# Second layer of a two-layer kernel: one of its Strassen products split by Strassen once more, and one sum formed by an adding DMA

## Chip, cores, metric

The kernel runs on one core of one Trainium2 chip. The time is device microseconds of one execution; before the change it is 2410.37 us, the median of 3 runs (2410.23 to 2410.72). The profile is one more execution of the same kernel, with a span of 2408.5 us on TensorE, VectorE (DVE in the profile), ScalarE (ACT), GpSimd (POOL) and the DMA queues.

## Reference

A causal depthwise convolution with 7 taps (softmax-normalised, one set for each of 8 heads), then a feed-forward layer with a hard-swish gate. All data is float32.

```python
batch, seq, d_model = (8, 4096, 192)         # 32768 tokens
d_ff = 2048

x = conv(x, softmax(weight))                 # (32768, 192)
h = x @ w_in                                 # (32768, 2048)   "first layer"
g = h * clip(h + 3.0, 0.0, 6.0) / 6.0        # the gate
out = g @ w_out                              # (32768, 192)    "second layer"
```

## The kernel before

The tokens go in 32 blocks of 1024. In a block the kernel keeps d_ff on the partitions, 16 chunks of 128. For the second layer it treats g as a 2 by 2 matrix: A11, A21, A12, A22 are d_ff half 0 or 1 (second digit) and token half 0 or 1 (first digit), each 8 chunks (NP) of 128 partitions by 512 tokens (N). w_out is a 2 by 2 matrix as well: d_ff halves by halves of the 192 output columns, 96 columns each, which are 3 column tiles (NQ) of 32 (QS). Strassen's scheme in Winograd's form makes 7 products of these quarters in place of 8, from sums S1 to S4 of the A and T1 to T4 of the B.

```python
g = cst.tile([P, NP, 2, G, N], F32, name="g")
g4 = g[:].rearrange("p c h k n -> p c (h k) n")
A11, A21, A12, A22 = (g4[:, :, j] for j in range(4))
S2, S3, S4 = A11, A21, A12                   # these sums are formed in place
psum = ps.tile([P, 2 * 4, N], F32, name="psum")     # 8 banks
...
def gate(out, r6, h):                        # L321, VectorE
    nc.vector.scalar_tensor_tensor(out=out, in0=r6, scalar=1.0, in1=h, op0=ALU.min, op1=ALU.mult)

def g_of(c, group, k):                       # where a gate writes
    return g[:, c, k, k if group == OWN else 1 - k]
```

The first layer (also in a Strassen form) runs in UNITS = 4 units of two chunks. A unit's steps stand in a plan as words: L or U is the lower or the upper half of the array (k = 0 or 1), P1 to P7 and K11 to K22 are matmuls, F1, CE, AF, AD copies and additions between PSUM banks, R a ReLU on ScalarE (L317), G a gate on VectorE (L321). The results of a unit are a and f (group OWN) and b and d (group OTHER), with a and b in chunk 2u and f and d in chunk 2u + 1. A step with ' belongs to the unit before, so that the fifth plan holds only what is left of unit 3.

```python
FIRST = """
    LP1 UP1 LP5 UP5 LF1 UF1 UP5+ LP6 LCE UCE UP6 LP2 UCE+ UK11 LAF LK11 UAF X UP2 LP7
    LRa UP7 LK12 URa LAD UP3 LP3 UAD LGa UK12 LK22 LRf UGa UK22 LK21 URf LGf LRd UK21
""".split()
...
OTHERS = """
    UP1 UGf' LP1 URd' LGd' LP4' UP4' UGd' LF1 LP5 UP5 UF1 LP6 UP6 LCE UCE LP2 UK11 LAF
    LRb' UAF LK11 UP2 URb' LGb' LP7 UP7 URa UGb' LRa LK12 UP3 LAD LP3 UAD UK12 UGa LK22
    UK22 LRf LGa URf LK21 UK21 LGf LRd
""".split()
PLANS = [FIRST, SECOND] + [OTHERS] * (UNITS - 1)

def h_phase(left):
    for u, plan in enumerate(PLANS):
        for step in plan:
            ...
        if u:
            g_sums(nc.gpsimd, (1, 3), range(2 * u - 2, 2 * u), 2)

def g_sums(engine, which, slots, width):     # L498
    forms = {
        1: (S1, A21, A22, ALU.add), 3: (S3, A11, A21, ALU.subtract),
        2: (S2, S1, A11, ALU.subtract), 4: (S4, A12, S2, ALU.subtract),
    }
    ...                                      # one tensor_tensor for each `width` chunks
```

The second layer. mm makes one matmul for each chunk (L437): the weights are 128x32, the array is split in 4 column tiles (j), and four such streams run side by side, one in each column tile.

```python
prod = {
    1: (A11, B11), 2: (A12, B21), 3: (S4, B22), 4: (A22, T4),
    5: (None, T1), 6: (S2, T2), 7: (S3, T3),
}                                            # product 5 reads S1

def side_by_side(*streams):
    for mms in zip(*streams):
        for m in mms:
            m()

def three(n, n4, q4):     # product n in column tiles 0 to 2, tile q4 of product n4 in the fourth
    return four(*[(n, q) for q in range(NQ)], (n4, q4))

def by_quarters(n, q):    # one column tile of a product, a quarter of its chunks in each j
    ...

def pieces(dst, q, src):  # and the sum of the quarters
    piece(dst, q, src, 0)                    # piece: a copy on ScalarE, L534
    for j in range(1, 4):
        add(dst[rows(q)], dst[rows(q)], src[rows(j)])     # add: VectorE, L542

def out_strassen(i, conv):
    p1, p2, p4, p5, u2, u3 = sums_tiles()
    for u in conv:                           # the next block's convolution, 7 taps on VectorE
        u()
    b, bank = three(1, 2, 0)
    nc.scalar.copy(out=p1[:], in_=bank[m])
    piece(p2, 0, bank, NQ)
    give(b)
    g_sums(nc.vector, (2,), every, 4)
    b, bank = three(4, 2, 1)
    nc.scalar.copy(out=p4[:], in_=bank[m])
    piece(p2, 1, bank, NQ)
    give(b)
    swap(slice(0, K3))
    b, bank = by_quarters(2, 2)
    pieces(p2, 2, bank)
    give(b)
    g_sums(nc.vector, (4,), every, 4)
    add(p2[:], p1[:], p2[:])
    store(i, p2, 0, 0)
    b7, bank7 = three(7, 5, 0)
    piece(p5, 0, bank7, NQ)
    y_sums()
    b, bank = three(6, 5, 1)
    ...                                      # p5, u2, u3, p4 from these banks, L542
    b, bank = three(3, 5, 2)
    ...
```

30 of the 32 blocks go through out_strassen; the first and the last have forms of their own (out_direct, out_last). The instructions of each engine run in the order of the program.

Of the kernel before, what the change touches and what calls it, by code (L numbers as in the profile page):

```python
# [8 lines left out]
ALU = mybir.AluOpType  # L9
ACT = mybir.ActivationFunctionType  # L10
AX = mybir.AxisListType
F32 = mybir.dt.float32
# [4 lines left out]
def kernel(  # L17
# [5 lines left out]
    moe_w_out: bass.AP,  # L23
    out: bass.AP,
):

# [10 lines left out]
    nc = tc.nc  # L39
    P = nc.NUM_PARTITIONS  # L40
# [6 lines left out]
    N = 512  # L47
# [11 lines left out]
    NP = NC // 2  # L59
    DH = D // 2  # L60
    QS = 32
    NQ = DH // QS
    assert NQ * QS == DH and NQ == 3 and P // QS == 4

    cst = ctx.enter_context(tc.tile_pool(name="cst", bufs=1))
# [25 lines left out]
    for base, dma in ((0, nc.scalar), (D2, nc.sync)):  # L91
        dma.dma_start(  # L92
            out=w_sb[base : base + D2],
            in_=weight.unsqueeze(1).to_broadcast([H, GJ, KC]),
# [24 lines left out]
    UNITS = NP // 2  # L119
# [3 lines left out]
    w_out = cst.tile([P, NP, 8, DH], F32, name="w_out")  # L123
    B11, B12, B21, B22, T1, T2, T3, T4 = range(8)
# [18 lines left out]
    def load_w_out(j):  # L143
# [3 lines left out]
        )  # L147
        return st

    EXP1 = 1 << 20  # L150
    bias_e = cst.tile([P, 2], F32, name="bias_e")
    nc.vector.memset(bias_e[:, 0:1], float((1023 - 127 + 255) * EXP1))
    nc.vector.memset(bias_e[:, 1:2], float(8 * 255 * EXP1))

# [58 lines left out]
    def w_sums():  # L213

        def sub(out, x, y):
            nc.gpsimd.tensor_tensor(out=out, in0=x, in1=y, op=ALU.subtract)

        for o, x, y in ((T1, B12, B11), (T3, B22, B12), (T2, B22, T1), (T4, T2, B21)):
            sub(w_out[:, :, o], w_out[:, :, x], w_out[:, :, y])
        b11, b12, b21, b22 = (w_in[:, c::2, s] for s in range(2) for c in range(2))  # L220
        t1, t2, t3, t4 = (w_in_t[:, j] for j in range(4))
        for o, x, y in ((t1, b12, b11), (t3, b22, b12), (t2, b22, t1), (t4, b21, t2)):
            sub(o, x, y)
# [3 lines left out]
    for n in range(AHEAD):  # L227
# [8 lines left out]
        out=e_sb[:], in0=w_sb[:], in1=mx[:].to_broadcast([P, KC]), op=ALU.subtract  # L236
# [9 lines left out]
    y = ys.tile([P, 2 * K3 + 4, N], F32, name="y")  # L246
# [26 lines left out]
    def swap(part):  # L273

        to = slice(OTHER + part.start, OTHER + part.stop)
        nc.sync.dma_start(out=y[D2:P, to], in_=y[0:D2, part])
        nc.sync.dma_start(out=y[0:D2, to], in_=y[D2:P, part])

    def y_sums():
        for o, a, b, op in (  # L280
            (YS1, OTHER, OTHER + 1, ALU.add), (YS3, OWN, OTHER, ALU.subtract),
            (YS2, YS1, OWN, ALU.subtract), (YS4, OWN + 1, YS2, ALU.subtract),
        ):
            nc.vector.tensor_tensor(out=y[:, o], in0=y[:, a], in1=y[:, b], op=op)
# [3 lines left out]
    g = cst.tile([P, NP, 2, G, N], F32, name="g")  # L288
    g4 = g[:].rearrange("p c h k n -> p c (h k) n")
    A11, A21, A12, A22 = (g4[:, :, j] for j in range(4))  # L290
    S2, S3, S4 = A11, A21, A12


    psum = ps.tile([P, 2 * 4, N], F32, name="psum")
    free_banks = list(range(2 * 4))

    def take():
        return free_banks.pop(0)

    def give(b):  # L300
        free_banks.append(b)
# [113 lines left out]
    def h_phase(left):  # L415
        work = {(u, k): Unit(u, k) for u in range(UNITS) for k in range(2)}
        for u, plan in enumerate(PLANS):
            for step in plan:
                if step == "X":
                    while left:  # L420
                        left.pop(0)()
                    continue
                op = step[1:].rstrip("'+")
                at = u + (step[-1] == "+") - (step[-1] == "'")
                if at < UNITS:
                    work[at, "LU".index(step[0])].run(op)
            if u:
                g_sums(nc.gpsimd, (1, 3), range(2 * u - 2, 2 * u), 2)

    def dff_half(k):  # L430
        return g[:, :, k // G, k % G]
# [1 line left out]
    def mm(bank, j, x, w, q, ps_, first, last, tokens=slice(0, N)):  # L433

        cols = slice(q * QS, (q + 1) * QS)
        return [
            lambda p=p: nc.tensor.matmul(  # L437
                out=bank[j * QS : (j + 1) * QS, tokens], lhsT=w_out[:, p, w, cols],
                rhs=x[:, p, tokens],
                start=(first and p == ps_[0]), stop=(last and p == ps_[-1]),  # L440
                tile_position=(0, j * QS),
            )
            for p in ps_
# [6 lines that stand above are left out]
# [38 lines left out]
    def g_sums(engine, which, slots, width):  # L488

        forms = {  # L490
            1: (S1, A21, A22, ALU.add), 3: (S3, A11, A21, ALU.subtract),
            2: (S2, S1, A11, ALU.subtract), 4: (S4, A12, S2, ALU.subtract),
        }
        for n in which:
            o, a, b, op = forms[n]
            for p in slots[::width]:
                r = slice(p, p + width)
                engine.tensor_tensor(out=o[:, r], in0=a[:, r], in1=b[:, r], op=op)  # L498
# [1 line left out]

    prod = {
        1: (A11, B11), 2: (A12, B21), 3: (S4, B22), 4: (A22, T4),
        5: (None, T1), 6: (S2, T2), 7: (S3, T3),
    }

    def product(bank, j, n, q, ks=every, **tokens):
        x, w = prod[n]
        return mm(bank, j, S1 if n == 5 else x, w, q, ks, True, True, **tokens)

    def four(*parts):  # L510

        b = take()
        bank = psum[:, b]
        side_by_side(*[product(bank, j, n, q) for j, (n, q) in enumerate(parts)])
        return b, bank

    def three(n, n4, q4):
        return four(*[(n, q) for q in range(NQ)], (n4, q4))

    def by_quarters(n, q):  # L520

        b = take()
        bank = psum[:, b]
        w = NP // 4
        side_by_side(
            *[product(bank, j, n, q, range(j * w, (j + 1) * w)) for j in range(4)]
        )
        return b, bank

    def rows(q):  # L530
        return slice(q * QS, (q + 1) * QS)

    def piece(dst, q, src, j):
        nc.scalar.copy(out=dst[rows(q)], in_=src[rows(j)])  # L534

    def pieces(dst, q, src):
        piece(dst, q, src, 0)
        for j in range(1, 4):
            add(dst[rows(q)], dst[rows(q)], src[rows(j)])

    def add(out, x, y, op=ALU.add):
        nc.vector.tensor_tensor(out=out, in0=x, in1=y, op=op)  # L542

    def store(i, c, k, half_, qs=range(NQ), queues=(nc.sync,), tokens=slice(0, N)):

        xt = ot.tile([P, N], F32, name="xt")
        r = slice(qs[0] * QS, (qs[-1] + 1) * QS)
        nc.vector.transpose(out=xt[r, tokens], in_=c[r, tokens])  # L548
        for q in qs:
            store_rows(i, k, half_ * NQ + q, xt, q, queues[q % len(queues)], tokens)  # L550

    def sums_tiles():
        return (cs.tile([DH, N], F32, name=f"c{k}") for k in range(6))

    m = slice(0, DH)
# [48 lines left out]
    def out_strassen(i, conv):  # L604
        p1, p2, p4, p5, u2, u3 = sums_tiles()
        for u in conv:
            u()
        b, bank = three(1, 2, 0)
        nc.scalar.copy(out=p1[:], in_=bank[m])  # L609
        piece(p2, 0, bank, NQ)  # L610
        give(b)
        g_sums(nc.vector, (2,), every, 4)
        b, bank = three(4, 2, 1)
        nc.scalar.copy(out=p4[:], in_=bank[m])  # L614
        piece(p2, 1, bank, NQ)
        give(b)
        swap(slice(0, K3))
        b, bank = by_quarters(2, 2)
        pieces(p2, 2, bank)
        give(b)  # L620
        g_sums(nc.vector, (4,), every, 4)
        add(p2[:], p1[:], p2[:])
        store(i, p2, 0, 0)
# [4 lines that stand above are left out]
        piece(p5, 1, bank, NQ)  # L628
        add(u2[:], p1[:], bank[m])
        give(b)  # L630
        add(u3[:], u2[:], bank7[m])
        give(b7)
        add(p4[:], u3[:], p4[:], ALU.subtract)
        store(i, p4, 1, 0)
        b, bank = three(3, 5, 2)
        piece(p5, 2, bank, NQ)
        add(u2[:], u2[:], bank[m])
        give(b)
        add(u2[:], u2[:], p5[:])
        store(i, u2, 0, 1)  # L640
        add(u3[:], u3[:], p5[:])
        return [lambda: store(i, u3, 1, 1)]
# [18 lines left out]
    with tc.manual_schedule():  # L661
# [4 lines left out]
            out=c_sb[:], in0=e_sb[:], in1=sm[:].to_broadcast([P, KC]), op=ALU.mult  # L666
# [14 lines left out]
        b = take()  # L681
        for _ in range(3):

            nc.tensor.matmul(
                out=psum[:, b], lhsT=zeros[:, 0:P], rhs=zeros[:], start=True, stop=True
# [57 lines left out]
        slots = [0, 1, 3, 4, 6, 7, 9, 10, 12, 13]  # L743
        n = 3
# [30 lines left out]
        ss = ctx.enter_context(tc.tile_pool(name="ss", bufs=1))  # L775
        p5s = ctx.enter_context(tc.tile_pool(name="p5s", bufs=3))
        cs = ctx.enter_context(tc.tile_pool(name="cs", bufs=1))
# [5 lines left out]
        out_direct(0, conv_and_swap(1))  # L783
        x_tiles[2] = load_x(2)

        S1 = ss.tile([P, NP, N], F32, name="s1")[:]
        left = []
        for i in range(1, NB):
            h_phase(left)
# [39 lines left out]
```

## Time and profile before

| What | Value |
|---|---|
| time, median of 3 | 2410.37 us |
| span of the profiled execution | 2408.5 us |
| first-layer matmuls (L311), busy | 885.2 + 524.8 us (w_in and its sums; two run side by side) |
| second-layer matmuls (L437), 512 tokens wide | 10736 records, mean 592 ns |
| gates on VectorE (L321) | 1024, mean 681 ns |
| ReLUs on ScalarE (L317) | 1024, mean 689 ns |
| convolution taps on VectorE (L263) | 186, mean 2179 ns |
| sum 1 on GpSimd (s<-g, L498) | 124, mean 2367 ns |
| sum 3 on GpSimd (g<-g, L498) | 124, mean 2730 ns |
| sums 2 and 4 on VectorE (L498) | 62 each, mean 2286 and 2289 ns |
| memory traffic | 24 GB/s over the span |

A matmul's own time (592 ns) is longer than the distance to the next one on the same part of the array, because matmuls are pipelined: lengths of stretches and starts are to be read, not sums of such times. The profile shows each fp32 matmul as two records. L numbers are lines of the kernel.

### The profile page before, as it was taken

The numbers are of one execution on the slowest core, as the hardware profiler recorded it, in microseconds if no ns is written. First come the engines' busy times: TensorE is split into PE (matmuls) and PEld (weight loads), VectorE is DVE, ScalarE is ACT, GpSimd is POOL, SyncE is SP. The second block draws the span as 40 slices with busy tenths as digits, with TensorE's granted clock in tenths as the row PEclk, the third lists the DMA queues.
The fourth block names the chain that finished last, engine by engine and source line by source line (L and its number), as shares of the span: only waits on it lengthen the run. The fifth ranks groups of instructions, "written<-read, shape, count | busy, mean of one in ns | idle before, by whom it ended". The sixth has DMA issues, their size and how long they took to land.

```text
span 2408.5 us, 40221 instructions
## 1 busy us (share of the span) xinstructions
PE 2400.5 (100%) x16536; PEld 1019.8 (42%) x16536; DVE 2089.4 (87%) x2533; ACT 1078.4 (45%) x1828; POOL 672.2 (28%) x280
## 2 busy tenths in 40 slices
PE   9999999999999999999999999999999999999999
PEld 5434444334444344443444434444344444344443
DVE  8788888988888888898888898888898888888896
ACT  7234553345543355433454334553345543355433
POOL 2423321233221333122332223322233312333122
PEclk9999999999999999999999999999999999999999
DMA  5211122101222011221112211122201122111210
GB/s 145 40 26 29 27 40 40 39 19 25 39 41 40 19 36 27 40 41 22 33 27 40 41 33 22 27 40 40 40 18 31 34 40 41 21 34 27 40 27 14
DMA packets 227400, 84.65 MB, mean 35 GB/s; under 512 B 205520, under 2 KB 210640, under 8 KB 227216
## 3 DMA queue, kind: packets, MB, share of 16 engines
q1 hardware_dynamic: 225880, 81.56, 17.2%
q8 instruction: 129, 2.11, 0.4%
q10 hardware_dynamic: 1240, 0.27, 0.1%
q14 instruction: 55, 0.45, 0.1%
q0 software_dynamic: 96, 0.26, 0.0%
HBM read 31.72 MB, written 25.17 MB: 24 GB/s over the span
## 4 chain that ended last, share of the span: by engine, by line
PE 99%; DVE 1%; DMA 0%; issue 0%; ACTq 0%; ACT 0%; DVEq 0%
PE psum L311 51%; PE psum L437 48%; DVE c L542 0%; DMA x<-in_x_dram 0%; DVE y L263 0%; DMA out_dram<-xt 0%; DVE xt L548 0%; DVE top L178 0%; ACTq L92 0%; PE psum L676 0%; DVE scale L174 0%; DVE y L259 0%; ACT c L534 0%; DVE scale L195 0%; DVEq L548 0%
## 5 line engine op out<-in xcount | busy, mean ns | idle before, releaser
L437 PE MATMUL psum<-g,w_out 128*32 128x512 f32 (+1 forms) x9376 | 1163.7, 590 | 0.0
L311 PE MATMUL psum<-y,w_in 64*128 64x512 f32 x3664 | 885.2, 591 | 0.6 <-POOL w_in L203 0.3
L498 POOL TENSOR_TENSOR s<-g 128x1024 f32<-128x1024 f32 x124 | 293.6, 2367 | 1644.5 <-DVE g L321 1644.5
L317 ACT ACTIVATE r<-psum,half 128x512 f32<-128x512 f32 x1024 | 642.1, 689 | 241.0 <-PE psum L311 233.9
L437 PEld LDWEIGHTS psum<-g,w_out 128*32 128x32 f32 x9376 | 339.5, 110 | 810.1 <-issue 765.7
L321 DVE SCALAR_TENSOR_TENSOR g<-r,psum 128x512 f32<-128x512 f32 x1024 | 641.6, 681 | 4.9 <-ACT r L317 1.9
L437 PE MATMUL psum<-s,w_out 128*32 128x512 f32 x1488 | 638.5, 592 | 0.0
L311 PEld LDWEIGHTS psum<-y,w_in 64*128 64x128 f32 x3664 | 437.1, 187 | 369.6 <-issue 290.6
L311 PE MATMUL psum<-y,w_in_t 64*128 64x512 f32 x1984 | 524.8, 592 | 0.0
L403 DVE TENSOR_TENSOR psum<-psum,p 128x512 f32<-128x512 f32 x496 | 324.6, 694 | 195.7 <-PE psum L311 186.8
L263 DVE SCALAR_TENSOR_TENSOR y<-x,c_sb,y 128x1536 f32<-128x1536 f32 (+1 forms) x206 | 414.3, 2018 | 6.6
L534 ACT COPY c<-psum 32x512 f32<-32x512 f32 x188 | 108.9, 579 | 600.5 <-PE psum L437 593.5
L498 POOL TENSOR_TENSOR g<-g 128x1024 f32<-128x1024 f32 x124 | 338.5, 2730 | 9.7
L311 PEld LDWEIGHTS psum<-y,w_in_t 64*128 64x128 f32 x1984 | 248.8, 186 | 192.9 <-issue 123.5
L542 DVE TENSOR_TENSOR c<-c,psum 32x512 f32<-32x512 f32 (+2 forms) x189 | 128.4, 679 | 81.2 <-ACT c L534 75.9
L396 ACT COPY psum<-psum 128x512 f32<-128x512 f32 x248 | 138.8, 571 | 72.4 <-PE psum L311 57.6
L437 PEld LDWEIGHTS psum<-s,w_out 128*32 128x32 f32 x1488 | 162.4, 110 | 1.2 <-issue 1.2
L399 ACT COPY p<-psum 128x512 f32<-128x512 f32 x248 | 133.2, 590 | 40.4 <-PE psum L311 39.5
L498 DVE TENSOR_TENSOR g<-s,g 128x2048 f32<-128x2048 f32 x62 | 139.3, 2286 | 3.9 <-POOL g L498 2.3
L498 DVE TENSOR_TENSOR g<-g 128x2048 f32<-128x2048 f32 x62 | 139.4, 2289 | 2.0 <-PE psum L437 1.0
L609 ACT COPY c<-psum 96x512 f32<-96x512 f32 x30 | 17.5, 582 | 174.6 <-PE psum L437 174.6
L614 ACT COPY c<-psum 96x512 f32<-96x512 f32 x30 | 17.5, 583 | 170.0 <-PE psum L437 170.0
(48 smaller groups left out, 438.3 us busy)
## 6 DMA issues: line engine op xcount, KB each, us to landing
out_dram<-xt SPq DMA_DIRECT2D x380, 64.0 KB, 2.0
y<-y SPq DMA_DIRECT2D x62, 384.0 KB, 4.9
x<-in_x_dram SPq DMA_DIRECT2D x55, 388.5 KB, 5.8
stage<-in_moe_w_in_dram SPq DMA_DIRECT2D x16, 192.0 KB, 4.5
stage<-in_moe_w_out_dram SPq DMA_DIRECT2D x8, 384.0 KB, 5.6
x<-in_x_dram SPq DMA_DIRECT2D x7, 384.0 KB
y<-y SPq DMA_DIRECT2D x6, 128.0 KB, 2.3
x<-in_x_dram SPq DMA_DIRECT2D x2, 128.0 KB, 4.5
```

What stands on the lines that cost most here:

```text
L263: nc.vector.scalar_tensor_tensor(out=to, in0=x[:, part, k + t : k + t + W], scalar=c, in1=to, op0=ALU.mult, op1=ALU.add,)
L311: nc.tensor.matmul(out=psum[:, b], lhsT=w[r], rhs=y[r, third_of_y], start=start, stop=stop, skip_group_check=onto,)
L317: nc.scalar.activation(r6, h, ACT.Relu, bias=half[:], scale=1.0 / 6.0)
L321: nc.vector.scalar_tensor_tensor(out=out, in0=r6, scalar=1.0, in1=h, op0=ALU.min, op1=ALU.mult)
L396: nc.scalar.copy(out=psum[:, bank["b"]], in_=psum[:, bank["a"]])
L399: nc.scalar.copy(out=self.p5[:], in_=psum[:, bank["e"]])
L403: nc.vector.tensor_tensor(out=psum[:, to], in0=psum[:, bank["b"]], in1=self.p5[:], op=ALU.add)
L437: lambda p=p: nc.tensor.matmul(out=bank[j * QS : (j + 1) * QS, tokens], lhsT=w_out[:, p, w, cols], rhs=x[:, p, tokens], start=(first and p ...
L498: engine.tensor_tensor(out=o[:, r], in0=a[:, r], in1=b[:, r], op=op)
L534: nc.scalar.copy(out=dst[rows(q)], in_=src[rows(j)])
L542: nc.vector.tensor_tensor(out=out, in0=x, in1=y, op=op)
L609: nc.scalar.copy(out=p1[:], in_=bank[m])
```

## The change

Product 1 is A11 B11. For two of the three column tiles of B11 it is split once more: A11 into token halves of 256 and alternate chunks (X11, X12, X21, X22), B11 into alternate chunks and the column tiles 0 and 1 (y11 to y22). Seven products of 4 chunks, 256 tokens and 32 columns stand for the eight. They fill the column tiles 0 and 1 of the first round (a11_round); the places that come free take a part of product 2, so that by_quarters becomes a shorter rest_of_2. The change is meant to take a little work from TensorE in each of 30 blocks.

It needs the sums of the X, four for each unit, on GpSimd (a11_sums), sums of the weights once at the start (w_q), and eight more VectorE additions in a block, which put the products together. To make room on GpSimd, S1 = A21 + A22 is no longer an instruction there: a DMA issued from GpSimd adds A22 onto A21 in place. S3, which lay there, moves to a buffer of its own.

```diff
-    S2, S3, S4 = A11, A21, A12
+    S2, S1, S4 = A11, A21, A12
...
             if u:
-                g_sums(nc.gpsimd, (1, 3), range(2 * u - 2, 2 * u), 2)
+                slots = slice(2 * u - 2, 2 * u)
+                g_sums(nc.gpsimd, (3,), range(NP)[slots], 2)
+
+                nc.gpsimd.dma_start(
+                    out=S1[:, slots], in_=A22[:, slots], accum_op=ALU.add
+                )
+            if u < UNITS:
+                a11_sums(u)
...
-        5: (None, T1), 6: (S2, T2), 7: (S3, T3),
+        5: (S1, T1), 6: (S2, T2), 7: (None, T3),          # product 7 reads S3
     }
+    TH = N // 2
+    first_half, second_half = slice(0, TH), slice(TH, N)
+    X11, X12, X21, X22 = (A11[:, c::2, t : t + TH] for t in (0, TH) for c in range(2))
+
+    def a11_sums(u):
+        s1, s2, s3, s4 = (sums[:, n, u] for n in range(4))
+        for o, a, b, op in (
+            (s1, X21[:, u], X22[:, u], ALU.add), (s3, X11[:, u], X21[:, u], ALU.subtract),
+            (s2, s1, X11[:, u], ALU.subtract), (s4, X12[:, u], s2, ALU.subtract),
+        ):
+            nc.gpsimd.tensor_tensor(out=o, in0=a, in1=b, op=op)
+
+    def quarters(dst, j, tokens, x, w):
+        return [
+            lambda u=u: nc.tensor.matmul(
+                out=dst[rows(j), tokens], lhsT=w[:, u], rhs=x[:, u],
+                start=(u == 0 and tokens == first_half), stop=(u == UNITS - 1),
+                tile_position=(0, j * QS), skip_group_check=True,
+            )
+            for u in range(UNITS)
+        ]
+
+    def a11_round(i, p1, p2):
+        ba, bb = take(), take()
+        a, b = (psum[:, n] for n in (ba, bb))
...
+        m0 = (
+            quarters(a, 0, first_half, X11, y11) + quarters(a, 0, second_half, s2, t2)
+            + quarters(b, 0, first_half, s3, t3) + quarters(b, 0, second_half, X12, y21)
+        )
+        m1 = (
+            quarters(a, 1, first_half, A12[:, ::2, first_half], w_out[:, ::2, B21, rows(2)])
+            + quarters(a, 1, second_half, s1, t1)
+            + quarters(b, 1, first_half, X22, t4) + quarters(b, 1, second_half, s4, y22)
+        )
+        m2, m3 = product(a, 2, 1, 2), product(a, 3, 2, 0)
+        for n in range(NP):
+            for mms, k in ((m0, 2 * n), (m1, 2 * n), (m2, n), (m3, n),
+                           (m0, 2 * n + 1), (m1, 2 * n + 1)):
+                mms[k]()
+        mp = cs.tile([P, TH], F32, name="mp")
+        r1, r2, r3 = (mp[rows(n)] for n in range(3))
+        nc.scalar.copy(out=r1, in_=a[rows(0), first_half])
+        piece(p1, 2, a, 2)
+        piece(p2, 0, a, 3)
+        add(r2, r1, a[rows(0), second_half])
+        add(p1[rows(0), first_half], r1, b[rows(0), second_half])
...                                          # five more additions of this size
+        give(bb)
+        return ba, a
+
+    def rest_of_2(a):
...
+        for p, tokens in ((1, slice(0, N)), (0, second_half)):
+            for j in range(4):
+                nc.tensor.matmul(
+                    out=bank[rows(j), tokens], lhsT=w[:, 2 * j + p],
+                    rhs=A12[:, 2 * j + p, tokens], start=bool(p), stop=True, ...
+                )
...
-        b, bank = three(1, 2, 0)
-        nc.scalar.copy(out=p1[:], in_=bank[m])
-        piece(p2, 0, bank, NQ)
-        give(b)
+        ba, a = a11_round(i, p1, p2)
...
-        b, bank = by_quarters(2, 2)
+        b, bank = rest_of_2(a)
         pieces(p2, 2, bank)
         give(b)
+        add(p2[rows(2), first_half], p2[rows(2), first_half], a[rows(1), first_half])
+        give(ba)
...
-        S1 = ss.tile([P, NP, N], F32, name="s1")[:]
+        S3 = ss.tile([P, NP, N], F32, name="s3")[:]
+        sums = ss.tile([P, 4, UNITS, N // 2], F32, name="sums")
```

More of the change, by code (lines that the diff above doesn't have):

```diff
@@ L148, in load_w_out @@
         return st
+    w_q = cst.tile([P, 4, UNITS, QS], F32, name="w_q")
     EXP1 = 1 << 20
@@ L219, in w_sums @@
             sub(w_out[:, :, o], w_out[:, :, x], w_out[:, :, y])
+        y11, y12, y21, y22 = (
+            w_out[:, c::2, B11, q * QS : (q + 1) * QS] for c in range(2) for q in range(2)
+        )
+        t1, t2, t3, t4 = (w_q[:, j] for j in range(4))
+        for o, x, y in ((t1, y12, y11), (t3, y22, y12), (t2, y22, t1), (t4, y21, t2)):
+            sub(o, x, y)
         b11, b12, b21, b22 = (w_in[:, c::2, s] for s in range(2) for c in range(2))
@@ L490, in g_sums @@
         forms = {
-            1: (S1, A21, A22, ALU.add), 3: (S3, A11, A21, ALU.subtract),
+            3: (S3, A11, A21, ALU.subtract),
             2: (S2, S1, A11, ALU.subtract), 4: (S4, A12, S2, ALU.subtract),
@@ new lines, in quarters @@
+    def quarters(dst, j, tokens, x, w):
[10 more added lines that the diff above has]
+        a, b = (psum[:, n] for n in (ba, bb))
+        y11, y12, y21, y22 = (
+            w_out[:, k::2, B11, q * QS : (q + 1) * QS] for k in range(2) for q in range(2)
+        )
+        t1, t2, t3, t4 = (w_q[:, n] for n in range(4))
+        s1, s2, s3, s4 = (sums[:, n] for n in range(4))
+        m0 = (
[6 more added lines that the diff above has]
+            + quarters(b, 1, first_half, X22, t4) + quarters(b, 1, second_half, s4, y22)
+        )
+        m2, m3 = product(a, 2, 1, 2), product(a, 3, 2, 0)
[10 more added lines that the diff above has]
+        add(p1[rows(0), first_half], r1, b[rows(0), second_half])
+        add(r3, r2, b[rows(0), first_half])
+        add(p1[rows(0), second_half], r3, b[rows(1), first_half])
+        add(p1[rows(1), second_half], r3, a[rows(1), second_half])
+        add(r2, r2, a[rows(1), second_half])
+        add(p1[rows(1), first_half], r2, b[rows(1), second_half])
+        give(bb)
+        return ba, a
@@ new lines, in rest_of_2 @@
+    def rest_of_2(a):
+        b = take()
+        bank = psum[:, b]
+        w = w_out[:, :, B21, rows(2)]
+        for p, tokens in ((1, slice(0, N)), (0, second_half)):
+            for j in range(4):
+                nc.tensor.matmul(
+                    out=bank[rows(j), tokens], lhsT=w[:, 2 * j + p],
+                    rhs=A12[:, 2 * j + p, tokens], start=bool(p), stop=True,
+                    tile_position=(0, j * QS), skip_group_check=True,
+                )
+        return b, bank
@@ L506, in product @@
     def product(bank, j, n, q, ks=every, **tokens):
         x, w = prod[n]
-        return mm(bank, j, S1 if n == 5 else x, w, q, ks, True, True, **tokens)
+        return mm(bank, j, S3 if n == 7 else x, w, q, ks, True, True, **tokens)
     def four(*parts):
```

## The prediction

> **What bounds the kernel now.** I read the page first: the share of each engine, then the chain that ended last, then that chain in order of time; after that, single stretches of one block in the timeline.
>
> ```profile
> PE 2400.5 (100%) x16536; PEld 1019.8 (42%) x16536; DVE 2089.4 (87%) x2533; ACT 1078.4 (45%) x1828; POOL 672.2 (28%) x280
> ...
> PE psum L311 51%; PE psum L437 48%; DVE c L542 0%; DMA x<-in_x_dram 0%; DVE y L263 0%; DMA out_dram<-xt 0%; DVE xt L548 0%; DVE top L178 0%; ACTq L92 0%; PE psum L676 0%; DVE scale L174 0%; DVE y L259 0%; ACT c L534 0%; DVE scale L195 0%; DVEq L548 0%
> ```
>
> TensorE carries 99% of the chain: half first layer (L311), half second (L437). VectorE is busy 87%, so it has little to spare. In order of time the chain alternates:
>
> ```profile
> 1177.99 36.19 PE psum L437 x336
> 1214.17 38.08 PE psum L311 x174
> 1252.25 36.19 PE psum L437 x336
> 1288.44 38.08 PE psum L311 x174
> ```
>
> One block of 1024 tokens is 38.08 + 36.19 = 74.27 us. A second layer has 42 steps in the code (three, three, by_quarters, three, three, three: 8+8+2+8+8+8), each of four matmuls side by side; 336 records over 4 column tiles are 84, so each fp32 matmul is two records, and a step of records costs 36.19/84 = 0.431 us.
>
> The last block already runs 256-token matmuls in four column tiles, so their price needs no guess:
>
> ```profile
> 2395.56 7.09 PE L437 MATMUL psum<-g,w_out 128*32 128x256 f32 x128
> ```
>
> and in the groups by form (the last figure but one is the mean, 379 ns):
>
> ```profile
> L437 PE MATMUL psum<-g,w_out 128*32 128x256 f32 x128 | 7.1, 379 | 0.0
> ```
>
> 128 records are 32 steps; (7.09 - 0.38)/31 = 0.2165 us each, against 0.431/2 = 0.2155. Halving the columns halves the time, and the weight loads stay hidden.
>
> What the other engines do where a second layer starts (TensorE's first L437 matmul is at 1252.18), ScalarE, VectorE and GpSimd, each from its own timeline:
>
> ```profile
> 1249.77 3.78 ACT L317 ACTIVATE r<-psum,half 128x512 f32<-128x512 f32 x6 [1.29 <-PE psum L311]
> ```
>
> ```profile
> 1252.29 2.00 DVE L321 SCALAR_TENSOR_TENSOR g<-r,psum 128x512 f32<-128x512 f32 x3
> 1254.20 1.81 DVE L259 TENSOR_SCALAR y<-x,c_sb 128x1536 f32<-128x1536 f32 x1
> ...
> 1289.12 0.68 DVE L542 TENSOR_TENSOR c<-c,psum 96x512 f32<-96x512 f32 x1 [2.15 <-ACT c L534]
> ```
>
> ```profile
> 1253.83 2.40 POOL L498 TENSOR_TENSOR s<-g 128x1024 f32<-128x1024 f32 x1 [1.51 <-DVE g L321]
> 1256.31 3.79 POOL L498 TENSOR_TENSOR g<-g 128x1024 f32<-128x1024 f32 x1
> ```
>
> The reader is to see three things. The gates of the last unit end only at 1252.29 + 2.00 = 1254.29, that is 2.11 us after the second layer has begun: ScalarE's six ReLUs run back to back behind the last first-layer matmuls. The second GpSimd sum took 3.79 us instead of its usual 2.37. And VectorE, from the convolution at 1254.20 on, has no idle time until it waits 2.15 us at the end of the second layer: that is its slack in this half of the block.
>
> **What the Trainium skill says.** "TensorE: Matmul & The Clock Gate", section "Part 3: Packing small matmuls — row/col tiling": matmuls start and end in strict order of the program, only weight loads are pulled ahead. So one matmul that waits for its data holds all behind it, in the other column tiles too. The trace agrees as far as it goes: starts within a step rise in order, 7 ns apart. "SBUF — State Buffer", section "Who interferes with whom": a VectorE instruction with two SBUF inputs and a GpSimd instruction that reads SBUF exclude each other for a whole instruction. The trace agrees: beside the 3.79 us sum one convolution tap took 3.82 us, the others 1.82; the gates, with one input in PSUM, slow no GpSimd sum (2.36 to 2.40). "DMA: Bandwidth & Descriptors", section "SWDGE vs HWDGE vs iDMA": a DMA that accumulates must be issued from GpSimd, where software writes the descriptors; its section "Anatomy of one DMA" fits 2.0 us + bytes/436 GB/s. By that an addition of 512 KB would land after about 3.2 us, an estimate for a plain copy; no run here shows an accumulating one.
>
> **The change part by part.**
>
> 1. TensorE work. The first round keeps its length: tiles 0 and 1 each get 16 half-width matmuls in place of 8 full ones: 32 record steps of 0.2165 = 6.93 us against 16 x 0.431 = 6.90, so +0.03. The seven half-width products of four chunks are 28 half matmuls instead of 32; the four free places take the even chunks of product 2, column tile 2, for the first token half. So by_quarters (2 steps, 4 record steps, 1.72 us) becomes a full step and a half one: 2 x 0.431 + 2 x 0.2165 = 1.30, so -0.43 us. Net -0.40 us a block, and 30 blocks go this way (the first and the last don't): **-12 us**. All of it lies on the path.
>
> 2. A new wait on TensorE. This is the step on which I decide the sign. Before, product 2 walked chunks 0 to 7 in order, so chunk 6 of A12 was wanted at its seventh step, 6 x 0.862 = 5.2 us into the round, long after its gate: UGb' of unit 3, the last of all, writes g[:, 6, 1, 0], which is that chunk, at 2.11. Now column tile 1 begins with chunks 0, 2, 4, 6 of A12 as its first four half matmuls: chunk 6 is wanted after three of them, 3 x 0.433 = 1.30 us. The gate is still written at 2.11: it follows the ReLU, that follows P4, the last matmul of the first layer, and none of these changes. With 0.06 us from VectorE to TensorE (an estimate: the last ReLU ends at 1253.55 and its gate starts at 1253.61) the wait is 2.11 + 0.06 - 1.30 = 0.87 us. Tile 1 has no hole later in which to catch up, and the order of the program holds the other tiles. 30 x 0.87 = **+26 us**.
>
> 3. The four sums of A11 on GpSimd (for unit 3 they are the late ones). By the 128x384 products (1.05 us) and the 128x1024 sums (2.37) one element costs 2.06 ns, so 256 elements 0.78 us, four 3.1. The gate they wait for (LGf) ends 1.0 us before the round; GpSimd is then free if the difference of unit 2 (2.4 us, from 1247.5 on, when the first sum of that unit starts now) and the DMA issue (two on GpSimd at the start took 0.69 and 0.52; estimated 1 to 2 us for four times the rows) are over, at -1.2 to -0.2. S2's part is then there 1.4 to 2.2 us into the round, wanted at 3.0 (3.9 with the wait of point 2). Hidden.
>
> 4. S1 by DMA. The last one is issued about 5 us into the round and read first by VectorE for S2 at about 20 us and by product 5 of the slots at about 21. Even three times the estimated landing fits. S1 in place of S3 as the sum in A21 blocks nothing: the next block writes A21 in its second unit. Hidden.
>
> 5. VectorE: eight more additions of 32x256 with one input in PSUM. The last block has two of that form at 425 ns; with 30 ns between them 8 x 0.455 = 3.6 us a block, 109 us in all. Against it: the first GpSimd sum no longer pushes the second into the convolution. Before, that cost a tap 2.0 us; now the one difference runs at 2.1 to 4.5 (up to 3.0 to 5.4 with a slow issue) and holds a tap from 3.87: 0.6 to 1.5 us. So VectorE is 2.2 to 3.1 us later at the end of the second layer. Its slack is 2.15, plus the 0.47 us by which TensorE itself comes later (0.87 - 0.40): 2.6. Hidden to 0.5 us too late; the additions L403 that follow feed a first-layer matmul with some 0.2 us to spare, so 0 to 0.3 us a block reach TensorE: 0 to 9 us, say **+3**. S2 and S4 come 2 to 3 us later and were 3.2 to 3.4 us early, so products 6 and 3 just don't wait.
>
> Sum: 2410.4 - 12 + 26 + 3 = **2427 us**, +0.7%.
>
> **The rivals.** (a) No new wait, the saving alone: 2398. For it: the trace shows no TensorE wait at all today, and two record steps less is certain. Against it: the order of chunks in the code and the end of the last gate, which is 2.11 us in the block shown. It needs TensorE to take the tiles out of order and catch up; tile 1 has no room. (b) VectorE becomes the bound: if its tap is still held for 2 us and the additions take 0.5 us, it is 4 us late instead of 2.6, TensorE waits another 1.2 us a block: +35, about 2460. For it: 87% busy and no hole for 33 us. Against it: the contention should fall, since one GpSimd sum less lies in the convolution. (c) GpSimd's descriptor writing is slow (4 us and more): then the sums of A11 are late and TensorE waits another 1 to 2 us: 2455 to 2485. For it: nobody has timed it here; against it: 0.5 to 0.7 us for 64 rows. (d) Mixed widths don't pack, each half step losing some: every 0.1 us a round is 3 us. Against it: the 256-wide steps above.
>
> **Range and chances.** The saving and the wait are both read from the trace within about 0.1 us a block (3 us). The uncertain rest is one-sided, VectorE and GpSimd up to +20, against a share of one in eight for rival (a). 2408 to 2446 should hold 8 in 10. Two per cent are 48 us: faster by that is out of reach of a 12 us saving; slower needs rival (b) or (c) in full.
>
> **What would show it.** In the chain in order of time the second layer should be about 36.65 us instead of 36.19, the first 38.1 to 38.4. In the timeline TensorE should stop 1.3 us into each second layer for 0.87 us, released by VectorE's gate (g, the line of L321), about 26 us in the list of waits. rest_of_2 should last 1.3 us. VectorE's busy time should be near 2089 + 102 - 35 = 2155 us, its idle time before the first addition after the second layer well under 1 us. If TensorE has no such stop, point 2 is wrong and 2398 is the time; if it stops on S2 or on sums of GpSimd, point 3; if the first layer grows, point 5.

## The result, and the profile after

The changed kernel takes 2423.84 us (median, 2423.76 to 2424.06), the kernel before 2410.3 us: a ratio of 1.0056, interval 1.0039 to 1.0074. It is 13.5 us slower. The prediction was 2427.

First the page of the changed kernel, busy times and the chain (line numbers have moved: L323 is now the first layer, L456 the matmuls of whole width, L545 those of a11_round, L598 rest_of_2, L333 the gates):

```profile
PE 2406.5 (99%) x17496; PEld 1105.3 (46%) x17496; DVE 2144.0 (89%) x2773; ACT 1089.2 (45%) x1858; POOL 836.5 (35%) x780
...
PE psum L323 51%; PE psum L456 40%; PE psum L545 4%; DVE g L333 2%; PE psum L598 1%; ACT r L329 1%; DMA x<-in_x_dram 0%; DMA out_dram<-xt 0%; DVE c L641 0%; DVE xt L647 0%; SPq L106 0%; SPq L140 0%; DVE top L184 0%; PE psum L774 0%; DVE y L275 0%
```

VectorE's gates and ScalarE's ReLUs, which were nowhere in the chain, now have 57 us of it, 2.4% (the page rounds to 2% and 1%). The chain in order of time shows where, once in each block, here around 1335 us:

```profile
1295.45 38.13 PE psum L323 x174
1333.58 0.68 ACT r L329
1334.26 0.02 issue
1334.28 1.30 DVE g L333 x2
1335.58 0.04 issue
1335.62 0.41 PE psum L545 x2
...
1341.20 7.08 PE psum L456 x62
1348.29 1.07 PE psum L598 x14
1349.36 20.82 PE psum L456 x190
1370.17 4.92 PE psum L323 x20
```

From 1333.58 on, for two microseconds, the end is not set by TensorE but by the last ReLU and the two gates behind it. The pieces of the chain don't begin and end exactly with the layers, so the lengths are read from TensorE's own starts: in this block the first layer goes from 1295.38 to 1333.46, 38.08 us as before, and the second from 1333.46 to 1370.11, 36.65 us in place of 36.19, the length that was predicted. The stop itself, in TensorE's timeline and the last two gates in VectorE's:

```profile
1334.36 0.60 PE L456 MATMUL psum<-g,w_out 128*32 128x512 f32 x2
1334.56 0.59 PE L545 MATMUL psum<-g,w_out 128*32 128x256 f32 x3
1334.78 0.60 PE L456 MATMUL psum<-g,w_out 128*32 128x512 f32 x2
1334.99 0.38 PE L545 MATMUL psum<-g,w_out 128*32 128x256 f32 x1
1335.62 0.40 PE L545 MATMUL psum<-g,w_out 128*32 128x256 f32 x1 [0.24 <-DVE g L333]
1335.63 0.40 PE L545 MATMUL psum<-sums,w_q 128*32 128x256 f32 x1
```

```profile
1334.28 1.29 DVE L333 SCALAR_TENSOR_TENSOR g<-r,psum 128x512 f32<-128x512 f32 x2
```

The gates end at 1335.57, and 0.05 us later all four column tiles go on at once. The figure in brackets is only the 0.24 us in which no matmul at all was running; what counts is the distance of starts. Column tile 1 started its last record before the stop 1.110 us after the start of the round and would have started the next one, the first of chunk 6, 0.216 us later, at 1.325; it started at 2.161. So the second layer stops for 0.836 us, and within 0.01 us the same in 29 of the 30 blocks.

What else the prediction had asked for: VectorE's wait at the end of the second layer, 2.15 us before, and GpSimd around the start of the round:

```profile
1370.86 0.68 DVE L641 TENSOR_TENSOR c<-c,psum 96x512 f32<-96x512 f32 x1 [0.54 <-ACT c L633]
```

```profile
1331.44 1.20 POOL L443 DMA_DIRECT2D g<-g  x1 [0.30 <-POOL s L517]
1332.55 1.55 POOL L537 TENSOR_TENSOR sums<-g 128x256 f32<-128x256 f32 x2
1333.92 0.87 POOL L537 TENSOR_TENSOR sums<-sums,g 128x256 f32<-128x256 f32 x1
1334.86 0.73 POOL L537 TENSOR_TENSOR sums<-g,sums 128x256 f32<-128x256 f32 x1
1335.55 2.40 POOL L517 TENSOR_TENSOR s<-g 128x1024 f32<-128x1024 f32 x1
```

VectorE still waits, but only 0.54 us. GpSimd has its last sum of the unit ready at 1335.59, before the matmul that wants it.

### The profile page after: what moved, and what is told of

Read it like the earlier page. It is cut to its first block, busy times and chain, and to the rows that moved or that the text cites. A ratio compares the mean times of both kernels' runs of the same rounds, so it can differ in the third digit from the quotient of the medians.

```text
span 2422.3 us, 43036 instructions
## 1 busy us (share of the span) xinstructions
PE 2406.5 (99%) x17496; PEld 1105.3 (46%) x17496; DVE 2144.0 (89%) x2773; ACT 1089.2 (45%) x1858; POOL 836.5 (35%) x780
## 3 DMA queue, kind: packets, MB, share of 16 engines
q8 instruction: 137, 2.24, 0.4%
## 4 chain that ended last, share of the span: by engine, by line
PE 96%; DVE 2%; ACT 1%; DMA 0%; issue 0%; SPq 0%; DVEq 0%; ACTq 0%
PE psum L323 51%; PE psum L456 40%; PE psum L545 4%; DVE g L333 2%; PE psum L598 1%; ACT r L329 1%; DMA x<-in_x_dram 0%; DMA out_dram<-xt 0%; DVE c L641 0%; DVE xt L647 0%; SPq L106 0%; SPq L140 0%; DVE top L184 0%; PE psum L774 0%; DVE y L275 0%
## 5 line engine op out<-in xcount | busy, mean ns | idle before, releaser
L456 PE MATMUL psum<-g,w_out 128*32 128x512 f32 (+1 forms) x7936 | 1148.2, 589 | 0.0
L323 PE MATMUL psum<-y,w_in 64*128 64x512 f32 x3664 | 885.0, 591 | 0.6 <-POOL w_in L209 0.4
L333 DVE SCALAR_TENSOR_TENSOR g<-r,psum 128x512 f32<-128x512 f32 x1024 | 641.8, 681 | 4.6 <-ACT r L329 1.5
L537 POOL TENSOR_TENSOR sums<-g 128x256 f32<-128x256 f32 x248 | 188.7, 835 | 1207.4 <-DVE g L333 1188.9
L323 PEld LDWEIGHTS psum<-y,w_in 64*128 64x128 f32 x3664 | 433.1, 187 | 373.8 <-issue 296.6
L456 PEld LDWEIGHTS psum<-g,w_out 128*32 128x32 f32 x7936 | 329.8, 110 | 445.8 <-issue 436.1
L323 PE MATMUL psum<-y,w_in_t 64*128 64x512 f32 x1984 | 524.4, 592 | 0.0
L415 DVE TENSOR_TENSOR psum<-psum,p 128x512 f32<-128x512 f32 x496 | 324.6, 694 | 195.8 <-PE psum L323 186.9
L633 ACT COPY c<-psum 32x512 f32<-32x512 f32 x218 | 126.3, 579 | 588.0 <-PE psum L456 577.2
L517 POOL TENSOR_TENSOR s<-g 128x1024 f32<-128x1024 f32 x124 | 293.7, 2368 | 244.2 <-PE psum L323 236.4
L275 DVE SCALAR_TENSOR_TENSOR y<-x,c_sb,y 128x1536 f32<-128x1536 f32 (+1 forms) x206 | 366.3, 1784 | 6.6
L323 PEld LDWEIGHTS psum<-y,w_in_t 64*128 64x128 f32 x1984 | 247.3, 186 | 194.3 <-issue 125.0
L517 DVE TENSOR_TENSOR g<-g 128x2048 f32<-128x2048 f32 x124 | 279.5, 2296 | 7.3 <-DMA g<-g 3.8
L456 PE MATMUL psum<-s,w_out 128*32 128x512 f32 x1488 | 230.3, 592 | 0.0
L443 POOL DMA_DIRECT2D g<-g x124 | 149.1, 1202 | 39.8 <-POOL s L517 39.8
L545 PE MATMUL psum<-g,w_out 128*32 128x256 f32 x720 | 132.6, 382 | 6.9 <-DVE g L333 6.9
L456 PEld LDWEIGHTS psum<-s,w_out 128*32 128x32 f32 x1488 | 73.7, 110 | 131.7 <-issue 124.3
L545 PE MATMUL psum<-sums,w_q 128*32 128x256 f32 x720 | 109.2, 380 | 0.0
```

Source lines behind the costliest of these rows:

```text
L275: nc.vector.scalar_tensor_tensor(out=to, in0=x[:, part, k + t : k + t + W], scalar=c, in1=to, op0=ALU.mult, op1=ALU.add,)
L323: nc.tensor.matmul(out=psum[:, b], lhsT=w[r], rhs=y[r, third_of_y], start=start, stop=stop, skip_group_check=onto,)
L415: nc.vector.tensor_tensor(out=psum[:, to], in0=psum[:, bank["b"]], in1=self.p5[:], op=ALU.add)
L443: nc.gpsimd.dma_start(out=S1[:, slots], in_=A22[:, slots], accum_op=ALU.add)
L456: lambda p=p: nc.tensor.matmul(out=bank[j * QS : (j + 1) * QS, tokens], lhsT=w_out[:, p, w, cols], rhs=x[:, p, tokens], start=(first and p ...
L537: nc.gpsimd.tensor_tensor(out=o, in0=a, in1=b, op=op)
```

## The experiments

The theory: the loss is the wait for the last gate, which the change moved forward in the round, and nothing else; the smaller amount of TensorE work is won. Rivals: the mixed widths cost it, the adding DMA or GpSimd costs it, VectorE's additions cost it.

### Chunk 6 late: the same matmuls in another order

```diff
         m1 = (
-            quarters(a, 1, first_half, A12[:, ::2, first_half], w_out[:, ::2, B21, rows(2)])
-            + quarters(a, 1, second_half, s1, t1)
-            + quarters(b, 1, first_half, X22, t4) + quarters(b, 1, second_half, s4, y22)
+            quarters(b, 1, first_half, X22, t4) + quarters(b, 1, second_half, s4, y22)
+            + quarters(a, 1, first_half, A12[:, ::2, first_half], w_out[:, ::2, B21, rows(2)])
+            + quarters(a, 1, second_half, s1, t1)
         )
```

> The changed kernel with column tile 1 of the first round in another order: the products of A11 first, the even chunks of A12 only from its ninth half matmul on, 4.7 us into the round (same matmuls, same sums). Theory (the loss is the wait for chunk 6 of A12, 0.84 us in each of 30 blocks): 2423.8 - 30 x 0.836 = 2399 us, up to 2402 if VectorE, now 0.3 us later than TensorE at the end of the second layer, makes the next first layer wait a little; no stop over 0.1 us in the first round. Rival 1 (the mixed widths or the larger number of matmuls cost the time): 2420 or more. Rival 2 (VectorE's eight additions or the adding DMA cost it): 2415 or more.

Measured: 2399.79 us (2399.71 to 2399.89); against the kernel before a ratio of 0.9956, interval 0.9941 to 0.9971. It beats both kernels. The chain of this version, in order of time:

```profile
1282.54 38.08 PE psum L323 x174
1320.62 0.34 PE psum L545 x2
...
1327.65 6.87 PE psum L456 x64
1334.52 1.29 PE psum L598 x16
1335.81 20.60 PE psum L456 x192
1356.41 18.75 PE psum L323 x84
```

Chunk 6 is the twelfth half matmul of its column tile here, wanted after eleven, 11 x 0.43 = 4.7 us. The second layer, 1320.62 to 1356.41, is 35.79 us, and between two first layers only TensorE stands in the chain. Nothing was taken out but the wait: same widths, same additions, same DMA. So both rivals fall, and 24.05 us, more than the whole loss, hung on where four half matmuls stand.

### The wait alone, in the kernel before

```diff
-        b, bank = three(1, 2, 0)
+        b = take()
+        bank = psum[:, b]
+        side_by_side(
+            *[product(bank, j, 1, j) for j in range(NQ)],
+            product(bank, NQ, 2, 0, (0, 6, 1, 2, 3, 4, 5, 7)),
+        )
```

> The kernel before, with one thing changed: product 2 in the first round takes its chunks in the order 0, 6, 1, 2, 3, 4, 5, 7. Theory: chunk 6 is then wanted 0.86 us into the round and is there at 2.17, so TensorE stops 1.3 us in each of 30 blocks: 2410.3 + 39 = 2449 us. Rival (TensorE lets the other column tiles go on and catches up, or the wait hides elsewhere): 2410 to 2420.

Measured: 2447.93 us (2447.7 to 2448.46), ratio 1.0156, interval 1.0141 to 1.0171: 37.6 us, or 1.25 us in each of the 30 blocks. In TensorE's timeline of this run the second layer begins at 1271.05 and goes on after its stop at 1273.21:

```profile
1271.05 1.92 PE L437 MATMUL psum<-g,w_out 128*32 128x512 f32 x14
1273.21 4.07 PE L437 MATMUL psum<-g,w_out 128*32 128x512 f32 x36 [0.24 <-DVE g L321]
```

1273.21 - 1271.05 = 2.16 us: the same moment after the start of the round as in the changed kernel, since it is the gate's. Only one of four column tiles needed chunk 6, and all four stood: 14 records had started, not more.

### Chunk 6 at the very start, in the changed kernel

```diff
-            quarters(a, 1, first_half, A12[:, ::2, first_half], w_out[:, ::2, B21, rows(2)])
+            quarters(a, 1, first_half, A12[:, ::2, first_half], w_out[:, ::2, B21, rows(2)],
+                     (3, 0, 1, 2))        # the order of the four
...                                          # quarters takes this order
```

> The changed kernel as it is, except that column tile 1 begins the first round with chunk 6 of A12, then 0, 2, 4. Theory: TensorE stops at once until the gate of chunk 6 is there, 2.16 us in place of 0.84: 2423.8 + 30 x 1.32 = 2463 us, and not more, since the 8 places later the order is the same. Rival (TensorE stops for the last gate wherever it stands in the round, or the stop is bound to something else, as the sums of GpSimd): 2424.

Measured: 2462.81 us (2462.71 to 2462.91), ratio 1.0217, interval 1.0187 to 1.0246. That is 39.0 us over the changed kernel, 1.30 us a block against 1.32 expected. In this kernel the place of chunk 6 in the round (0, 1.3 and 4.7 us after its start) so gives 2463, 2424 and 2400 us: the time follows the wait, and once the gate is early enough nothing more is won.

### The adding DMA alone, in the kernel before

```diff
-    S2, S3, S4 = A11, A21, A12
+    S2, S1, S4 = A11, A21, A12
...
-                g_sums(nc.gpsimd, (1, 3), range(2 * u - 2, 2 * u), 2)
+                slots = slice(2 * u - 2, 2 * u)
+                g_sums(nc.gpsimd, (3,), range(NP)[slots], 2)
+                nc.gpsimd.dma_start(
+                    out=S1[:, slots], in_=A22[:, slots], accum_op=ALU.add
+                )
...                                          # S3's buffer, products 5 and 7 as in the change
```

> The kernel before, with only the second part of the change: S1 by the adding DMA in place of A21, S3 in a buffer of its own, product 1 not split. Theory (the DMA is off the path): 2410 us within 1, VectorE's busy time lower by some 50 us (its convolution is no longer held for 2 us a block). Rival (the adding DMA costs something by its issue or its landing): 2413 or more.

Measured: 2410.81 us (2410.12 to 2411.3), ratio 1.0001, interval 0.9993 to 1.001. The busy times of the page, then the convolution in the groups by form (busy time, mean ns of one, idle time before it):

```profile
PE 2400.5 (100%) x16536; PEld 1021.0 (42%) x16536; DVE 2029.7 (84%) x2533; ACT 1078.2 (45%) x1828; POOL 482.5 (20%) x280
```

```profile
L263 DVE SCALAR_TENSOR_TENSOR y<-x,c_sb,y 128x1536 f32<-128x1536 f32 x186 | 345.6, 1858 | 6.6
```

A convolution tap takes 1858 ns instead of 2179, and VectorE's busy time falls by 59.7 us; the time doesn't move, since none of it was on the path. The DMA costs nothing that this comparison can show, and it frees VectorE.

### The reordered version, S1 back on GpSimd

```diff
-                g_sums(nc.gpsimd, (3,), range(NP)[slots], 2)
-
-                nc.gpsimd.dma_start(
-                    out=S1[:, slots], in_=A22[:, slots], accum_op=ALU.add
-                )
+                g_sums(nc.gpsimd, (3, 1), range(NP)[slots], 2)
...
+            1: (S1, A21, A22, ALU.add), ...
```

> As the run with the even chunks late, but S1 again by an instruction on GpSimd (in place of A21, after S3) and not by DMA. Theory: GpSimd has 1.2 us more to do in each unit where it is already late; the last sums of A11 come about 0.4 us too late for TensorE, and two sums instead of one lie in the convolution, so that VectorE is 3 to 4 us later: 2460 to 2500 us. Rival (the DMA is a convenience): the time of the run with the even chunks late, within 3 us.

Measured: 2483.5 us (2483.2 to 2483.6), ratio 1.0303, interval 1.0286 to 1.032: 83.7 us over the reordered version, 2.8 us a block. GpSimd's two sums lie beside the convolution from 1367.94 to 1374.18, and the second takes 3.77 us, as in the kernel before. Six taps of the convolution in VectorE's timeline:

```profile
1368.82 14.40 DVE L275 SCALAR_TENSOR_TENSOR y<-x,c_sb,y 128x1536 f32<-128x1536 f32 x6
```

The same six taps in the reordered version:

```profile
1324.42 11.49 DVE L275 SCALAR_TENSOR_TENSOR y<-x,c_sb,y 128x1536 f32<-128x1536 f32 x6
```

14.40 - 11.49 = 2.91 us later, and 2.8 of them reach the end. In the list of waits TensorE waits for VectorE's sums (L513), not for GpSimd's:

```profile
PEld psum L452 <- DVE g L513: 102.0, 60, 2.5
```

So one of the two causes that I had expected did the work: the late sums of A11 cost TensorE nothing that this list shows, and no two starts in its first round are more than 0.45 us apart. Put beside the run before it: in the kernel before, holding the convolution for 2 us cost nothing; here, 2.9 us cost 2.8. The DMA is no convenience once VectorE has eight additions more.

### How much slack VectorE has left in the reordered version

```diff
+        for _ in range(8):                 # and 3 in the second run
+            add(mp[rows(3)], r1, a[rows(0), second_half])
         give(bb)
         return ba, a
```

> The version with the even chunks late, with eight more VectorE additions of 32x256 beside the seven that put product 1 together; they write a place that nobody reads, so the output stays what it is, and only VectorE's work grows, by 8 x 0.445 = 3.6 us a block. Theory (VectorE's slack of 2.15 us in the second layer is spent; what is added now reaches TensorE in full): 2399.8 + 30 x 3.3 to 3.6 = 2499 to 2507 us. Rival (VectorE is busy 89% and idle some 8 us a block, so it absorbs them, and the run with S1 on GpSimd was slow for the late sums): 2400 to 2415.

Measured: 2516.01 us (2515.78 to 2516.23), ratio 1.0437, interval 1.0407 to 1.0468. The rival with idle time to absorb them is out, but the loss is 9 us over the upper end of my range. TensorE's timeline of one block, then two stretches of it (columns: stretch, its length, busy time and number on PE, PEld, DVE, ACT, POOL, granted share of TensorE's clock, DMA share, GB/s):

```profile
470.01 0.60 PE L456 MATMUL psum<-s,w_out 128*32 128x512 f32 x2
472.87 3.19 PE L456 MATMUL psum<-g,w_out 128*32 128x512 f32 x13 [2.26 <-DVE g L517]
```

```profile
473.34:476.75 3.41, 3.41 (x24) 0.87 (x20) 3.31 (x4) 0.00 (x0) 0.00 (x0) 0.50 0.00 0
627.50:630.90 3.40, 2.01 (x20) 0.68 (x24) 3.40 (x2) 0.00 (x0) 0.00 (x0) 1.00 0.02 5
```

TensorE stops before product 6 for S2 (L517). In this block the granted clock is halved 0.47 us after it has gone on, and for 3.41 us; after a stop of the same length in the block around 626 us it is not (the last section says what differed). The clock record has 18 such stretches beside the one at the end. Most blocks without one take 77.34 to 77.38 us (from stop to stop, as 626.06 to 703.40), that is 3.47 more than the 73.87 of the reordered version, for 3.56 us of additions; most with a halved clock take 77.95 to 78.03. 30 x 3.47 + 18 x 0.65 = 115.8 us; measured are 116.2. So my range was too low by what the clock took, which it had left out. The second run was made to see the slack without it:

> The version with the even chunks late and three more VectorE additions of 32x256 that nobody reads: 3 x 0.445 = 1.34 us of VectorE a block. With eight more, TensorE stopped 2.4 us before product 6 and its clock was halved afterwards in some blocks, which blurs what VectorE's lateness alone costs; with three the stop is too short for that. Theory A (no slack at all is left on VectorE): 2399.8 + 30 x 1.2 to 1.34 = 2436 to 2440 us. Theory B (some 0.7 us is left, as the run with eight gives if 30 us of its loss are the clock): 2399.8 + 30 x 0.64 = 2419 us, the larger part of it in the next first layer, whose additions L415 then come late.

Measured: 2437.33 us (2437.3 to 2437.46), ratio 1.0111, interval 1.0094 to 1.0128: 37.5 us over the reordered version, 1.25 us a block for 1.34 us of additions, as theory A said. The waits that have grown (PEld, for the first matmul after the wait):

```profile
PEld psum L456 <- DVE g L517: 57.6, 60, 1.3
...
PEld psum L323 <- DVE psum L415: 27.2, 65, 0.6
```

In the reordered version the first of them is not in the list and the second is 11.7 us. VectorE's lateness reaches TensorE at three places, at S2, at S4 and at the additions L415 of the next first layer. By TensorE's starts the second layers are 0.52 us longer than in the reordered version and the first layers 0.73 (means of 30 blocks), so the larger part does come in the next first layer.

## Why the prediction was right

**Step 1, TensorE's work.** Predicted -0.40 us a block. The reordered version, without the wait, goes through a block in 73.866 us (from first layer to first layer), the kernel before in 74.264: -0.40. rest_of_2 was put at 1.30 us and takes 1.29. The half widths pack as the last block had shown.

**Step 2, the wait.** Predicted: chunk 6 wanted at 1.30 us, its gate written at 2.11, TensorE on again at 2.17, a wait of 0.87. Measured: 1.325, 2.107, 2.161, a wait of 0.836: 25 us in 30 blocks against 26. The list of waits, where I had looked for 26 us, has only 6.9 on PE for these gates, since it counts the stretches in which no matmul was running. The runs with chunk 6 late, second and first move this term alone: the first loses nothing, the second 1.25 us a block in a kernel that had no wait, and the third 1.30 more than the 0.84. This cause is shown. The word of the Trainium skill on which it rests ("TensorE: Matmul & The Clock Gate", section "Part 3: Packing small matmuls — row/col tiling": the order of the program is kept) holds here: one tile's missing chunk stopped all four.

**Step 3, the sums on GpSimd.** One was put at 0.78 us and took 0.73 to 0.84; S2's last part was to be there 1.4 to 2.2 us into the round and is there at 1.33. Hidden, as predicted.

**Step 4, the DMA.** The issue, estimated 1 to 2 us, is 1.20; the landing, estimated 3.2 us from the Trainium skill's fit for copies ("DMA: Bandwidth & Descriptors", section "Anatomy of one DMA"), has a median of 5.0 us here, for a transfer that also adds:

```profile
g<-g POOLq DMA_DIRECT2D x124, 512.0 KB, 5.0
```

The margin held in the 30 blocks: the last addition had landed 6.3 us or more before S2 began. In the last block, which I had left out because product 1 isn't split there, it was used up: without a convolution ahead of it VectorE's S2 waits for the DMA.

```profile
DVE g L517 <- DMA g<-g: 3.8, 1, 3.8
```

This wait cost next to nothing. Counted from the first second-layer matmul of the last block, TensorE's last matmul starts after 35.92 us in both kernels, and VectorE's last instruction ends after 39.65 us before and 39.67 now. The last block still takes 42.71 us instead of 42.14, but this difference lies behind VectorE's end, where the last store to out_dram lands after 41.79 us instead of 41.22; no run says why.

**Step 5, VectorE.** An addition was put at 0.455 us with its gap and takes 0.445. The tap that GpSimd's sum holds took about 2.22 us in most blocks instead of 1.82, so 0.4 lost; I had 0.6 to 1.5. VectorE so comes 2.07 us later, where I had 2.2 to 3.1, and keeps 0.54 us of its wait. Nothing of the +3 us that I had put down reached TensorE: by its starts the first layers take 38.08 us in both kernels. (The 38.13 of the chain above is where the chain leaves TensorE, not a longer layer.) This is the term that was too large: the saving of 12 us and a wait of 25 make 13 us, and measured are 13.5. The taps are also the main reason why VectorE is busy 2144 us and not 2155: their time fell by 405.4 - 357.3 = 48 us, where I had taken 35.

**The rivals.** (a), 2398 without the wait, is the time of the reordered version to within 2 us, but got by taking the wait away, not by TensorE working round it. (b), VectorE as the bound, did not come true for the change, but lies next: with the wait removed, 1.34 us more on VectorE cost 1.25. (c) and (d) fell with the numbers above.

## What to carry to other kernels

When a product is cut up, look at which chunk of its input is written last and when, and place the matmul that reads it as late in the round as the order allows: with matmuls in program order, one early reader stops every column tile, and here the place of four half matmuls decided between 13.5 us lost and 10.6 us won. A saving on the bounding engine that adds work to a neighbour uses up that neighbour's slack; read the slack in the stage, not from the share of busy time: in the reordered version VectorE was 89% busy and had almost none left. A DMA that adds can take an elementwise sum off an engine for its issue alone (here 1.20 us of GpSimd in place of 2.37), if its landing has several microseconds of room.

## What the runs showed of the hardware that was not expected

- In the run with eight more additions TensorE ran no matmul for 1.9 to 2.6 us before product 6, once in each of 30 blocks, and in 18 of them the granted clock was then halved for 3.41 us. The beginnings of these 18 stretches are 78.51 or 232.11 us apart, 23 or 68 times 3.413 us, so they lie on one grid. Laid over TensorE's timeline, it separates the blocks: every step of 3.413 us in which no matmul ran for 2.17 us or more was followed by a halved one, and no step with 1.96 us or less was. The stop at 626 us, 2.24 us without a matmul, fell over the edge of a step, with 1.96 us in the one and 0.29 in the other. This is one profile, and no run moves a stop against the grid to test it. In the other runs the longest time without a matmul between the first block and the last was 1.55 us, and the clock stayed at full speed there.
- A halved clock for 3.41 us is 1.7 us of TensorE's work, and made a block some 0.65 us longer. That VectorE, the bound in that run, hid the rest is likely but not shown.
- The adding DMA of 512 KB between places of SBUF occupied GpSimd for 1.20 us at each of 124 issues, also while convolution taps ran on VectorE, and landed after a median of 5.0 us (5.0 to 6.7); in the run with this DMA alone the taps beside its issue kept their 1.82 us.
